# Queueing each PSUM eviction of the second-stage groups with the group's last product instead of with the next unit of work

## The chip, the cores and the metric

One core of a Trainium2 chip. The kernels of the first four experiments ran on one chip and those of the last on another, each beside the kernel before. The metric is the device time of one launch in microseconds, of which several runs are given. All runs quoted here are of the fast state.

## The reference, cut to what matters

Softcapped attention (batch 8, 12 heads, 448 rows, head size 64), followed by a two-branch maximum and an output product:

```python
scores = cap * np.tanh(scale * np.matmul(q, k.transpose(0, 1, 3, 2)) / cap)   # cap = 30
attn = np.exp(scores - max) / sum
x = np.matmul(attn, v)  ->  (3584, 768)
g = np.maximum(x @ w1, x @ w2)          # w1, w2: (768, 1024)
out = g @ w_out                         # w_out: (1024, 768)
```

The kernel uses max(a, b) = max(a - b, 0) + b: `g` becomes relu(x @ (w1 - w2)), and x @ w2 @ w_out is added through a premultiplied matrix `wm`.

## The kernel before

TensorE writes its products into banks of the memory called PSUM. A *group* is the products that are summed up in one bank, and its *eviction* is the VectorE instruction that copies the sum out, after which the bank can take another group. In the listings `esum` holds sums of exponentials, `xT` the result of attention, `gT` the relu results and `osb` finished output rows; `st`, `rs` and `inv` are the three steps from the softmax sum to its inverse.

The kernel interleaves two stages. The first (attention) keeps ScalarE busy with tanh and exp. The second (`moe`) is pure matrix work and fills the gaps of TensorE: it is a Python generator, and `F(n)` takes n products from it wherever the first stage leaves room. All engines get their instructions in the order in which the Python code records them.

```python
mm_psum = ctx.enter_context(tc.tile_pool(name="mm_psum", bufs=2, space=PSUM))   # two banks for "mm"
...
def moe(b):
    ...
    for f in range(FC):                                  # 8 groups of 6 products
        ps = mm_psum.tile([P, 512], f32, name="mm")
        for c in range(KC):
            nc.tensor.matmul(ps[:, :S], wd_sb[:, c, ...], x[:, c, cs], ...)      # L399
            yield
        nc.vector.tensor_relu(g[:, f, cs], ps[:, :S])                            # L403, the eviction
    for t in ...:
        for half in range(2):                            # groups of 14 products
            ps = mm_psum.tile([P, 512], f32, name="mm")
            ...                                          # L411 and L414, a yield after each product
            nc.vector.tensor_copy(osb[:, hs], ps[:, : DM // 2])                  # L418, the eviction
...
def F(n):
    rate[1] += n * rate[0]
    while rate[1] >= 1 and fill_q:
        try:
            next(fill_q[0])
            rate[1] -= 1
        except StopIteration:
            fill_q.pop(0)
...
for t in range(1, NQ):                                   # one pass is about 12 us
    ...                                                  # F, scores, exp, additions to esum
    F(3); add(t, 0, 2)
    F(4); add(t, 1, 2)
    F(8)
    scores(t + 1, 2); ex(t + 1, 1)
    total(t)                 # PE L350: sum of esum; VectorE: st L352, rs, inv
    normalize(t, values(t))  # PE L366/L372: v; VectorE: two multiplications to xT, L387
    F(9)
```

The `yield` comes after each product. So after the last product of a group the generator pauses, and the eviction is recorded only when the next unit is taken: behind whatever the loop has recorded for VectorE between two calls of `F`. This happens only where a group's last product is also the last of a call of `F`.

## Time and profile before

| | before |
|---|---|
| median of 3 runs | 347.99 us (347.97 to 348.53) |
| span of the profiled run | 345.9 us |
| TensorE (PE) busy | 94% |
| ScalarE (ACT) busy | 80% |
| VectorE (DVE) busy | 66% |

How to read it: PE is the busiest engine, so what counts is the time in which PE stands still. The prediction below shows the lines for that. Two more views carry the argument. The first is what ACT waited for from 210 us to 302 us in the kernel before (us in total, times, longest): it has gaps, so it follows PE and does not lead it.

```profile
ACT tanh L304 <- PE s L303: 3.4, 6, 1.3
ACT tanh L304 <- PE s L300: 0.2, 1, 0.2
```

The second is PE's timeline near 175 us in the kernel before (start, length, what, count).

```profile
173.47 4.76 PE L399 MATMUL mm<-xT,wd_sb 128*128 128x448 bf16 x22
```

22 products at 189 ns each, the last one shown with its 353 ns, would be 21 x 0.189 + 0.353 = 4.32 us. It takes 4.76, so some 0.44 us are stalls within one line that shows no idle mark. By the starts of the single records they are 0.145 us at 175.32 and 0.284 us at 177.87. I call this "lost time": the distance between the starts of two products less 189 ns (448 columns) or 163 ns (384).

The same measure finds another loss, which is no wait for an eviction. In the kernel before PE passes 116 times from 72 us to the end between products of form 128\*128 and products of form 64\*128 or 128\*32, and each time 92 to 96 ns are lost without an idle mark: 10.9 us in all, about three times the stalls that this document is about. No experiment here touches them.

### The profile page before, as it was taken

The page shows a single profiled execution, that of the slowest core. Times are in us where ns is not written, and L with a number is a line of the kernel's source. Part 1 is how long each engine was busy: PE and PEld are TensorE (multiplying, and loading weights), DVE is VectorE, ACT ScalarE, POOL GpSimd, SP SyncE. Part 2 cuts the span into 40 slices and gives each one's busy share as a digit, 9 for nine tenths or more (in the row PEclk, how much of TensorE's full clock was granted, in tenths as well). Part 3 has the DMA queues.
Part 4 walks back from the last instruction along what each step waited for, and adds up shares of the span by engine and source line. Part 5 has one row for each costly group of instructions (what it writes and reads, how often), then busy time and mean ns, then how long its engine had stood idle before and what let it go on. Part 6 is the DMA issues. An engine that isn't in the chain of part 4 may idle for free.

```text
span 345.9 us, 6777 instructions
## 1 busy us (share of the span) xinstructions
PE 326.2 (94%) x2710; PEld 163.3 (47%) x2710; DVE 227.4 (66%) x410; ACT 277.2 (80%) x241; POOL 109.8 (32%) x172
## 2 busy tenths in 40 slices
PE   3669979999999999999999999999999999999996
PEld 1324545445544554455444454454445554555563
DVE  5324645886777767777687768767776777874421
ACT  3998939989999999899999999799989999900000
POOL 6653848542144134304413431341343040000000
PEclk9959999999999999999999999999999999999999
DMA  7999999997695969775985499839956921012032
GB/s 253 252 253 242 369 204 180 247 213 199 132 295 158 211 149 282 205 172 123 252 252 100 134 230 300 179 96 216 307 124 143 209 96 46 2 47 91 0 93 91
DMA packets 103200, 61.78 MB, mean 179 GB/s; under 512 B 62337, under 2 KB 98177, under 8 KB 103169
## 3 DMA queue, kind: packets, MB, share of 16 engines
q1 hardware_dynamic: 101216, 58.21, 65.1%
q0 software_dynamic: 1952, 3.15, 5.0%
q8 instruction: 21, 0.34, 0.4%
q14 instruction: 11, 0.08, 0.1%
HBM read 42.47 MB, written 11.01 MB: 155 GB/s over the span
## 4 chain that ended last, share of the span: by engine, by line
PE 80%; DMA 13%; DVE 5%; issue 1%; SPq 0%; DVEq 0%
PE mm L414 22%; PE mm L399 19%; PE mm L411 16%; DMA kr<-in_k_dram 9%; PE v L366 6%; PE s L303 6%; DMA qkT<-kqf 3%; PE v L303 2%; PE s L300 2%; PE v L372 2%; PE mm L243 2%; PE s L350 2%; DMA osb<-in_moe_w_dram 1%; DVE xT L387 1%; DVE gT L403 1%; DVE st L352 1%
## 5 line engine op out<-in xcount | busy, mean ns | idle before, releaser
L309 ACT ACTIVATE expo<-tanh 128x2688 bf16<-128x2688 bf16 (+1 forms) x72 | 140.3, 1950 | 0.8 <-PE v L366 0.6
L304 ACT ACTIVATE tanh<-s 128x896 bf16<-128x896 f32 x122 | 106.4, 914 | 24.3 <-PE s L303 20.2
L414 PE MATMUL mm<-wo_sb,gT 128*128 128x384 bf16 x448 | 85.8, 327 | 0.0
L399 PE MATMUL mm<-xT,wd_sb 128*128 128x448 bf16 x384 | 78.8, 353 | 1.9 <-DVE gT L403 1.4
L411 PE MATMUL mm<-wm_sb,xT 128*128 128x384 bf16 x336 | 66.0, 326 | 0.4 <-DVE gT L403 0.4
L414 PEld LDWEIGHTS <-gT 128*128 128x128 bf16 x448 | 42.3, 98 | 34.7 <-issue 8.5
L418 DVE COPY osb<-mm 128x384 f32<-128x384 f32 x56 | 31.1, 555 | 40.7 <-PE mm L414 40.3
L399 PEld LDWEIGHTS <-wd_sb 128*128 128x128 bf16 x384 | 35.8, 98 | 41.2 <-issue 11.0
L403 DVE TENSOR_SCALAR gT<-mm 128x448 bf16<-128x448 f32 x64 | 39.4, 622 | 17.7 <-PE mm L399 17.2
L628 POOL COPY mark<-inv 1x1 f32<-1x1 f32 x18 | 3.2, 177 | 141.0 <-DVE inv L356 125.7
L411 PEld LDWEIGHTS <-xT 128*128 128x128 bf16 x336 | 31.7, 98 | 25.9 <-issue 5.9
L304 ACT ACTIVATE tanh<-v 128x896 bf16<-128x896 f32 x46 | 42.5, 923 | 0.0
L366 PE MATMUL v<-expo,vp 128*32 128x448 bf16 x576 | 35.6, 353 | 0.0
L303 PE MATMUL s<-qkT 64*128 64x448 bf16 x196 | 29.1, 371 | 6.7 <-ACT tanh L304 3.1
L387 DVE TENSOR_TENSOR xT<-v,inv 128x448 bf16<-128x448 f32 x48 | 27.8, 620 | 4.4 <-PE v L372 2.0
L352 DVE STREAM_TRANSPOSE st<-s 128x448 f32<-128x448 f32 x24 | 15.6, 650 | 19.8 <-PE s L350 17.5
L329 DVE TENSOR_TENSOR esum<-expo 128x896 bf16<-128x896 bf16 x42 | 27.9, 665 | 0.0
L327 DVE TENSOR_TENSOR esum<-esum,expo 64x896 bf16<-64x896 bf16 x42 | 26.6, 633 | 1.3
L331 DVE TENSOR_TENSOR esum<-esum,expo 128x896 bf16<-128x896 bf16 x42 | 26.7, 637 | 1.0
L303 PEld LDWEIGHTS <-qkT 64*128 64x128 bf16 x288 | 10.6, 96 | 29.7 <-issue 21.3
L366 PEld LDWEIGHTS <-vp 128*32 128x32 bf16 x576 | 15.3, 97 | 10.0
L183 POOL CAST kqf<-kr 128x1152 bf16<-128x1152 f32 x14 | 15.9, 1137 | 10.5 <-DMA kr<-in_k_dram 10.3
(66 smaller groups left out, 257.1 us busy)
## 6 DMA issues: line engine op xcount, KB each, us to landing
kr<-in_k_dram SPq DMA_DIRECT2D x14, 576.0 KB, 7.2
qr<-in_q_dram SPq DMA_DIRECT2D x14, 576.0 KB, 7.0
vr<-in_v_dram SPq DMA_DIRECT2D x14, 576.0 KB, 4.9
out_dram<-osb SPq DMA_DIRECT2D x20, 384.0 KB, 3.5
out_dram<-osb SPq DMA_DIRECT2D x16, 192.0 KB, 3.3
osb<-in_moe_w_dram SPq DMA_DIRECT2D x4, 512.0 KB, 8.6
gT<-in_moe_w_dram POOLq DMA_DIRECT2D x6, 256.0 KB, 12.8
wo_sb<-in_moe_w_out_dram POOLq DMA_DIRECT2D x4, 384.0 KB, 16.0
```

What stands on the lines that cost most here:

```text
L303: nc.tensor.matmul(s[:, m, :S], k0[r, j * P : (j + 1) * P], qTn[r, :])
L304: nc.scalar.activation(tanh[t, p][:, 2 * j : 2 * j + 2, :], s[:, :, :S], AF.Tanh, scale=scale / cap)
L309: nc.scalar.activation(expo[t, p], tanh[t, p][:, 0:n, :], AF.Exp, scale=float(cap))
L329: nc.vector.tensor_add(d, e_of(t, ab, 0), e_of(t, ab, 1))
L331: nc.vector.tensor_add(d, d, e_of(t, ab, 2))
L366: nc.tensor.matmul(ps[r, :S], vp[g % 2][:, 2 * n + h, j, u::2], e_of(t, ab, j)[:, h, :], start=(j == 0), stop=False,)
L387: nc.vector.tensor_mul(x_of(t, u), ps[:, u, :S], inv[t])
L399: nc.tensor.matmul(ps[:, :S], wd_sb[:, c, f * P : (f + 1) * P], x[:, c, cs], start=(c == 0), stop=(c == KC - 1))
L403: nc.vector.tensor_relu(g[:, f, cs], ps[:, :S])
L411: nc.tensor.matmul(ps[:, : DM // 2], x[:, c, ts], wm_sb[:, c, hs], start=(c == 0), stop=False)
L414: nc.tensor.matmul(ps[:, : DM // 2], g[:, f, ts], wo_sb[:, f, hs], start=False, stop=(f == FC - 1))
L418: nc.vector.tensor_copy(osb[:, hs], ps[:, : DM // 2])
```

## The change

Its intent: the eviction is recorded together with the group's last product, so that VectorE can empty the bank as soon as the group is done. The same edit is made in the three generators; the core of it:

```diff
     def moe(b):
+        yield
         ...
         for f in range(FC):
-            ps = mm_psum.tile([P, 512], f32, name="mm")
             for c in range(KC):
+                if f + c > 0:
+                    yield
+                if c == 0:
+                    ps = mm_psum.tile([P, 512], f32, name="mm")
                 nc.tensor.matmul(...)
-                yield
             nc.vector.tensor_relu(g[:, f, cs], ps[:, :S])
     ... (the same in turn_w2, premultiply and the second half of moe)
     def F(n):
         rate[1] += n * rate[0]
         while rate[1] >= 1 and fill_q:
+            g = fill_q[0]
+            if g is not rate[2]:
+                rate[2] = g
+                next(g)
+            rate[1] -= 1
             try:
-                next(fill_q[0])
-                rate[1] -= 1
+                next(g)
             except StopIteration:
                 fill_q.pop(0)
```

More of the change, by code (lines that the diff above doesn't have):

```diff
@@ L229, in turn_w2 @@
     def turn_w2(c):
-        ps = mm_psum.tile([P, 512], f32, name="mm").bitcast(bf16)
         for f in range(FC):
+            yield
+            if f == 0:
+                ps = mm_psum.tile([P, 512], f32, name="mm").bitcast(bf16)
             nc.tensor.transpose(ps[:, f * P : (f + 1) * P], w2b[:, c, f * P : (f + 1) * P], ident)
-            yield
         w2T[c] = stage.tile([P, FC * P], bf16, name="w2T", bufs=2)
@@ L240, in premultiply @@
             hs = slice(half * (DM // 2), (half + 1) * (DM // 2))
-            ps = mm_psum.tile([P, 512], f32, name="mm")
             for f in range(FC):
+                yield
+                if f == 0:
+                    ps = mm_psum.tile([P, 512], f32, name="mm")
                 nc.tensor.matmul(
@@ L246, in premultiply @@
                 )
-                yield
             nc.vector.tensor_copy(wm_sb[:, c, hs], ps[:, : DM // 2])
@@ L391, in moe @@
     def moe(b):
+        yield
         if b % 2 == 0:
@@ L396, in moe @@
         for f in range(FC):
-            ps = mm_psum.tile([P, 512], f32, name="mm")
             for c in range(KC):
+                if f + c > 0:
+                    yield
+                if c == 0:
+                    ps = mm_psum.tile([P, 512], f32, name="mm")
                 nc.tensor.matmul(
@@ L401, in moe @@
                 )
-                yield
             nc.vector.tensor_relu(g[:, f, cs], ps[:, :S])
@@ L408, in moe @@
                 hs = slice(half * (DM // 2), (half + 1) * (DM // 2))
-                ps = mm_psum.tile([P, 512], f32, name="mm")
                 for c in range(KC):
+                    yield
+                    if c == 0:
+                        ps = mm_psum.tile([P, 512], f32, name="mm")
                     nc.tensor.matmul(ps[:, : DM // 2], x[:, c, ts], wm_sb[:, c, hs], start=(c == 0), stop=False)
+                for f in range(FC):
                     yield
-                for f in range(FC):
                     nc.tensor.matmul(
@@ L416, in moe @@
                     )
-                    yield
                 nc.vector.tensor_copy(osb[:, hs], ps[:, : DM // 2])
@@ L440 @@
     fill_q = []
-    rate = [1.0, 0.0]
+    rate = [1.0, 0.0, None]
     def F(n):
```

## The prediction

> **What bounds the kernel now.** I read first the page's busy table and slices (which engine is full, and when), then the waits of TensorE (what it stands still for), then the timeline of TensorE and VectorE around its longest wait, and then that of two smaller stalls which the wait view hides.
>
> ```profile
> PE 326.2 (94%) x2710; PEld 163.3 (47%) x2710; DVE 227.4 (66%) x410; ACT 277.2 (80%) x241; POOL 109.8 (32%) x172
> ...
> PE   3669979999999999999999999999999999999996
> ...
> DVE  5324645886777767777687768767776777874421
> ACT  3998939989999999899999999799989999900000
> ```
>
> TensorE (PE) is at 9 tenths or more from the fourth slice on but for the sixth and the last; VectorE (DVE), which does the evictions, is at about two thirds. ScalarE (ACT) is nearly as full as PE until about 302 us and then has nothing left, while PE goes on alone for 43 us. So the end is set by PE's total work plus every time PE stands still. Where does it stand still after the start? This is the view of PE's waits from 56 us to the end:
>
> ```profile
> PE mm L399 <- DVE gT L403: 1.4, 3, 0.8
> PE mm L411 <- DVE gT L403: 0.4, 1, 0.4
> PE mm L399 <- DVE xT L387: 0.2, 1, 0.2
> ```
>
> The columns are us in total, times, longest. Two microseconds in 290: that is about all that an earlier eviction could buy, and the change can only take the part that comes from the place of an eviction in the queue. The longest is at 217.75 us. First PE, then DVE, from the timeline (start, length, engine, line, count):
>
> ```profile
> 209.92 3.57 PE L399 MATMUL mm<-xT,wd_sb 128*128 128x448 bf16 x18
> 213.33 0.54 PE L300 MATMUL s<-qkT 128*128 128x448 bf16 x2
> 213.80 0.37 PE L350 MATMUL s<-esum,ones 128*32 128x448 bf16 x4
> ...
> 215.62 1.31 PE L399 MATMUL mm<-xT,wd_sb 128*128 128x448 bf16 x6
> 217.75 0.73 PE L399 MATMUL mm<-xT,wd_sb 128*128 128x448 bf16 x3 [0.82 <-DVE gT L403]
> ```
>
> ```profile
> 212.57 0.62 DVE L403 TENSOR_SCALAR gT<-mm 128x448 bf16<-128x448 f32 x1
> 214.23 0.65 DVE L352 STREAM_TRANSPOSE st<-s 128x448 f32<-128x448 f32 x1 [1.03 <-PE s L350]
> 214.91 0.24 DVE L354 RECIPROCAL rs<-st 128x14 f32<-128x14 f32 x1
> 215.26 0.65 DVE L356 STREAM_TRANSPOSE inv<-rs 128x448 f32<-128x448 f32 x1
> 216.01 1.16 DVE L387 TENSOR_TENSOR xT<-v,inv 128x448 bf16<-128x448 f32 x2
> 217.08 1.15 DVE L403 TENSOR_SCALAR gT<-mm 128x448 bf16<-128x448 f32 x2
> ```
>
> A group of L399 has 6 products. The 18 from 209.92 are three whole groups, the third of them done at 209.92 + 3.57 = 213.49. VectorE then idles 1.03 us and does not evict it: the eviction was not yet on its queue, because the generator had paused after the sixth product. The four steps of the softmax sum and the two multiplications come first, and the eviction is the first of the pair at 217.08, 3.59 us late. There are two banks for "mm", so the six products from 215.62 use the other bank, and the seventh stands still until 217.75.
>
> **What the Trainium skill says.** "PSUM — Partial Sum Buffer", section "Engine vs sequencer instructions": VectorE's queue is strict first in, first out, so a place in the queue is a place in time. The trace agrees: done at 213.49, evicted at 217.08, with VectorE idle in between. The same page, "PSUM bank collisions raise a hardware error": TensorE must not write a bank while it is read, and software guards that, so the next but one group's first product waits for the eviction. The trace agrees: eviction over at 217.70 (half of 1.15 us after 217.08, with a few hundredths of overlap), product at 217.75. "TensorE: Matmul & The Clock Gate", section "Step-by-step: what each phase is for": products in a row are N/2.4 + 2.5 ns apart, so 189 ns for 448 columns and 162.5 for 384. The trace agrees: starting at 209.92 and 213.33, 18 products take 3.41 us, 189 ns each. "Perfetto Trace Analysis", section "Identifying the Most-Contended Engine": matmul busy time is a bad measure because matmuls are pipelined. Here too: the stall shows as 0.82 us idle, but the seventh product was due 189 ns after the sixth, whose shown length is 353 ns (the L399 row's mean), so PE lost 0.82 + 0.353 - 0.189 = 0.98 us.
>
> **The change part by part.** It adds no instruction: it moves the `yield` from after a product to before it, so that one step of the generator now ends behind the group's last product and takes the eviction with it. The budget counts as before: a generator's first step is now free, and its end falls into its last paid step. I built both kernels and laid their instruction orders side by side. PE, ACT, POOL and SP have the same instructions in the same order; so output stores and input loads do not change places. On VectorE 123 of 136 evictions stand where they stood. 13 move forward: 12 of them ahead of one `esum` addition (0.62 us each), and one, of a gT group, ahead of the five steps from st to xT. That one is the eviction above.
>
> - *The one at 217.08.* Its group is done at 213.49. The eviction before it (212.57) will run slightly later, as another gT eviction moves ahead of an addition and waits for its group until 211.22: eviction 211.26 to 211.88, two additions to about 213.06, the eviction of 212.57 until about 213.65, and ours until about 214.2, about when st could start before (214.23). So it fits into the idle 1.03 us. The bank is free at 214.2 and wanted at 215.62 + 6 x 0.189 = 216.75. The stall vanishes: 217.75 - 216.75 = 1.0 us, 0.98 by the reckoning above.
> - *Two gT evictions at 174.65 and 295.36.* Both groups are done 0.44 us before their evictions start, because VectorE is in an addition. In the second, VectorE and then PE:
>
> ```profile
> 294.82 0.62 DVE L331 TENSOR_TENSOR esum<-esum,expo 128x896 bf16<-128x896 bf16 x1
> 295.36 1.35 DVE L403 TENSOR_SCALAR gT<-mm 128x448 bf16<-128x448 f32 x2
> ```
>
> ```profile
> 294.17 3.15 PE L399 MATMUL mm<-xT,wd_sb 128*128 128x448 bf16 x15
> ```
>
>   15 products would take 14 x 0.189 + 0.353 = 3.00 us and take 3.15, so PE lost 0.15. With the eviction ahead of L331 it starts at about 294.96 and that is won: the group that can then start earlier is evicted at 297.92, and no product waits for that. At 174.65 the same 0.15 would be won, but is given back: two groups on, PE waits for the eviction of 177.20, which stands behind two additions in both kernels. Net 0.
> - *The ten others* (eight of osb, two of gT). Each starts within 0.04 to 0.64 us of its group's end, and its bank is wanted 0.3 to 3.8 us after it is over. No PE time hangs on them: 0.
> - *Stalls that stay*: those at 68.2, 73.3, 95.7 to 96.3, 145.4 and 177.9 belong to evictions or xT steps which do not move.
>
> Sum: 0.98 + 0.15 = 1.13 us. It carries to the end only if nothing else binds behind 217 us. ACT's waits there speak for it: it waits for PE 3.6 us in 7 pieces, the longest (1.3 us) for just the product that comes 0.98 us earlier; PE never waits for ACT in that stretch. So ACT moves along. From 220 to 302 us PE shows 82.00 of 82.00 us busy. 347.99 - 1.13 = 346.9 us.
>
> **The rivals.** (1) *The early eviction blocks.* In 11 of the 13 moves the eviction has to wait for a group which ends after the addition could have started (by only 0.1 us in two of them); at 87.2, 196.4 and 244.6 the addition started 1.9, 1.6 and 1.7 us before the eviction, and will now come after it. If that pushed the softmax sum, PE's L350 would wait. Against it: behind each such move there is idle time before the next hard date (0.77, 1.27, 0.76 us in these three, against one addition of 0.62), and the sum's last addition is done 0.4 us or more before L350 wants it at 190.3, 238.6 and 262.9; only at 308.3 is it about 0.1 us. If I am wrong in one or two places, 0.2 to 0.6 us are lost, and the result is 347.3 to 347.9. (2) *ACT or a transfer takes over the bound.* If ACT had no slack, the 0.98 us would only become a wait of PE for a score bank, and would be given back: 347.8. ACT's waits speak against it; so do the key and query transposes, issued at 219.6 and landed 5.5 us later, while their scores come a pass of 12 us later. (3) *Much more comes out*, because evictions as such hold PE up: then 340 or less. The waits speak against it: all of them together are 2 us as shown, and 3.7 by the reckoning with 189 ns.
>
> **Range and chances.** Only 1.13 us is at stake and runs of one kernel spread by 0.5 us (347.97 to 348.53). I take 346.9, range 346.0 to 347.9: the low end allows for a spread of that size and a little more won; the high end is everything given back. Two per cent would be 7 us, more than all stalls behind 56 us: faster 0.01, within 2% 0.98, slower 0.01.
>
> **What would show it.** PE's waits behind 90 us should lose their entry of 0.8 us; the seventh L399 product near 217.7 should follow the sixth in one run without an idle mark. A gT eviction should stand at about 213.6, before st. The run of 15 near 293 should take 3.00 us. PE's busy time should hardly change and the span fall by 1.1 us. A new wait of PE for esum (L350), or a wait of PE for tanh, would prove me wrong, and so would a st that starts later against PE's products.

## The result, and the profile after

| | before (one run more than above) | after |
|---|---|---|
| median | 348.26 us (347.97 to 348.86, 4 runs) | 347.07 us (346.88 to 347.16, 4 runs) |
| ratio of fast runs | | 0.9963, 95% interval 0.9946 to 0.998 |
| span of the profiled run | 345.9 us | 345.3 us |

Ratios here are those of the record, from the fast runs, and not quite the ratio of the medians quoted. The change is worth 1.2 us by the medians; the interval of the ratio allows 0.7 to 1.9 us.

The changed kernel's lines are numbered differently: L399 became L405, the eviction L403 became L408, L411 and L414 became L418 and L421, st is L354, the sum L352. PE's waits from 56 us to the end, after:

```profile
PE mm L405 <- DVE gT L408: 0.7, 2, 0.4
PE mm L418 <- DVE gT L408: 0.4, 1, 0.4
PE mm L405 <- DVE xT L389: 0.2, 1, 0.2
```

The entry of 0.8 us is gone. Two smaller differences hide in the first line: 0.26 us near 178 us are new (see below), and the 0.18 us that were marked at 68.19 us before are missing. The latter is not the change's doing, as the first eviction that moves stands at 87 us: the lost time at that product was between 0 and 0.48 us in the eight traces of this case. The stretch in which the 0.8 us lay, PE and then DVE in the timeline of the changed kernel:

```profile
210.51 3.57 PE L405 MATMUL mm<-xT,wd_sb 128*128 128x448 bf16 x18
213.91 0.54 PE L302 MATMUL s<-qkT 128*128 128x448 bf16 x2
...
216.21 1.88 PE L405 MATMUL mm<-xT,wd_sb 128*128 128x448 bf16 x9
```

```profile
212.38 1.26 DVE L329 TENSOR_TENSOR esum<-esum,expo 64x896 bf16<-64x896 bf16 x2
213.68 1.16 DVE L408 TENSOR_SCALAR gT<-mm 128x448 bf16<-128x448 f32 x2
214.81 0.65 DVE L354 STREAM_TRANSPOSE st<-s 128x448 f32<-128x448 f32 x1
```

What stood as 6 products, a stall and 3 products is one run of 9: 8 x 0.189 + 0.353 = 1.87 us are expected and 1.88 shown. The eviction is the second of the pair at 213.68; VectorE has no idle time left before st, so it fits in with nothing to spare. The run of 15 that took 3.15 us in the kernel before takes 3.01, with its eviction at 294.56 ahead of the addition; the run of 22 near 174 us keeps a stall, and that one now has an idle mark of its own:

```profile
293.78 3.01 PE L405 MATMUL mm<-xT,wd_sb 128*128 128x448 bf16 x15
```

```profile
174.05 4.15 PE L405 MATMUL mm<-xT,wd_sb 128*128 128x448 bf16 x21
178.46 0.35 PE L405 MATMUL mm<-xT,wd_sb 128*128 128x448 bf16 x1 [0.26 <-DVE gT L408]
```

21 products without a stall are 20 x 0.189 + 0.353 = 4.13 us: the first stall is gone. The second lost 0.284 us before and loses 0.425 now, so 0.141 of the 0.145 us that the first one won were given back.

**Why the two profiles' spans differ by 0.6 us only.** The start of a run varies: the 601st of PE's 2710 matmul records began at 72.00 us in the profile before and at 72.59 in the one after, on the same instructions. The traces show where the 0.59 us come from. The granted TensorE clock, at half in both, came back to full at 27.53 us before and only at 29.42 after. These are the same two products, before and then after; by their single records their starts are 189 and 374 ns apart:

```profile
27.98 0.54 PE L300 MATMUL s<-qkT 128*128 128x448 bf16 x2
```

```profile
28.36 0.95 PE L302 MATMUL s<-qkT 128*128 128x448 bf16 x2
```

Just before the stall near 68 us PE was 0.91 us behind, and 0.32 us of it were won back at that stall. What sets the moment at which the clock comes back is not shown. From the 601st record to the start of the last it is 270.16 us before and 269.03 after: 1.12 us less (differences of this kind are taken before rounding), where 1.13 were predicted. In what follows I call this stretch "from the 601st product on". It is the sharper measure: in the second trace of the changed kernel, on another occasion, it was 269.03 us again.

### The profile page after: what moved, and what is told of

It reads as the page before. It is cut to its first block, busy times and chain, and to the rows that moved or that the text cites. A ratio compares the mean times of both kernels' runs of the same rounds, so it can differ in the third digit from the quotient of the medians.

```text
span 345.3 us, 6777 instructions
## 1 busy us (share of the span) xinstructions
PE 326.7 (95%) x2710; PEld 163.6 (47%) x2710; DVE 226.5 (66%) x410; ACT 277.1 (80%) x241; POOL 107.8 (31%) x172
## 3 DMA queue, kind: packets, MB, share of 16 engines
q0 software_dynamic: 1952, 3.15, 5.0%
## 4 chain that ended last, share of the span: by engine, by line
PE 81%; DMA 13%; DVE 4%; issue 0%; SPq 0%; DVEq 0%
PE mm L421 22%; PE mm L405 20%; PE mm L418 16%; DMA kr<-in_k_dram 9%; PE v L368 6%; PE s L305 6%; DMA qkT<-kqf 3%; PE v L305 2%; PE s L302 2%; PE v L374 2%; PE mm L246 2%; PE s L352 2%; DMA osb<-in_moe_w_dram 2%; DVE xT L389 1%; DVE gT L408 1%; DVE st L354 1%
## 5 line engine op out<-in xcount | busy, mean ns | idle before, releaser
L421 PE MATMUL mm<-wo_sb,gT 128*128 128x384 bf16 x448 | 85.8, 327 | 0.0
L405 PE MATMUL mm<-xT,wd_sb 128*128 128x448 bf16 x384 | 78.3, 353 | 1.0 <-DVE gT L408 0.7
L418 PE MATMUL mm<-wm_sb,xT 128*128 128x384 bf16 x336 | 66.1, 327 | 0.4 <-DVE gT L408 0.4
L421 PEld LDWEIGHTS <-gT 128*128 128x128 bf16 x448 | 42.3, 98 | 34.7 <-issue 8.5
L405 PEld LDWEIGHTS <-wd_sb 128*128 128x128 bf16 x384 | 35.8, 98 | 39.6 <-issue 8.6
L408 DVE TENSOR_SCALAR gT<-mm 128x448 bf16<-128x448 f32 x64 | 39.3, 621 | 16.9 <-PE mm L405 16.7
L418 PEld LDWEIGHTS <-xT 128*128 128x128 bf16 x336 | 31.7, 98 | 25.9 <-issue 5.9
L354 DVE STREAM_TRANSPOSE st<-s 128x448 f32<-128x448 f32 x24 | 15.6, 649 | 16.3 <-PE s L352 14.0
```

Of the source, the lines that this page charges most:

```text
L405: nc.tensor.matmul(ps[:, :S], wd_sb[:, c, f * P : (f + 1) * P], x[:, c, cs], start=(c == 0), stop=(c == KC - 1))
L418: nc.tensor.matmul(ps[:, : DM // 2], x[:, c, ts], wm_sb[:, c, hs], start=(c == 0), stop=False)
L421: nc.tensor.matmul(ps[:, : DM // 2], g[:, f, ts], wo_sb[:, f, hs], start=False, stop=(f == FC - 1))
```

## The experiments

The kernels below were built so that PE, ACT, POOL and SP have the same instructions in the same order as before; only VectorE's order differs, and the traces show the same. For the first three I put every eviction into a function which either records it at once, or at the next unit as before (`LATE`), or after `normalize` of the same pass (`HOLD`). Evictions are numbered as they are recorded. With all 13 moved ones in `LATE` every engine's order, as built, is that of the kernel before; with none it is that of the changed kernel (neither was run). In these kernels L447 is L399, L450 is the eviction L403 and L460 is L411. The edit, shortened:

```diff
-            nc.vector.tensor_relu(g[:, f, cs], ps[:, :S])
+            evict(lambda f=f, ps=ps: nc.vector.tensor_relu(g[:, f, cs], ps[:, :S]))
+    def evict(f):
+        n = count[0]; count[0] += 1
+        if n in LATE: waiting.append(f)      # recorded when the next unit is taken
+        elif n in HOLD: held.append(f)       # recorded after normalize(t, ...)
+        else: f()
```

The theory is that of the prediction: an eviction's place costs PE time only where its bank is wanted before the eviction is over, and of the 13 moves one wins 0.98 us, one 0.15, one wins 0.15 and loses it again, and ten nothing. The main rival is that evicting earlier helps a little everywhere.

### One move alone

```diff
+    LATE = {27, 53, 62, 69, 71, 76, 87, 89, 98, 105, 111, 116}    # all that moved but number 78
```

> Theory (one eviction pays): this is the kernel before with only the single gT eviction moved that stood behind the five steps from st to xT. PE's 0.8 us wait for L403 near 217 us goes, the others stay, and the time falls by 0.98 us: ratio to before 0.997. Rival (evictions at the group's end help in general, a little at each of 13 places): one of 13 gives about 0.1 us, ratio 0.9997.

Measured: 347.40 us median of 17 runs, before 348.43 of 30 on the same chip; ratio 0.9973, interval 0.9962 to 0.9983. From the 601st product on it took 269.18 us, 0.97 less than the kernel before. PE's waits from 56 us on:

```profile
PE mm L447 <- DVE gT L450: 0.4, 1, 0.4
PE mm L460 <- DVE gT L450: 0.4, 1, 0.4
PE mm L447 <- DVE xT L406: 0.2, 1, 0.2
```

The 0.8 us entry is gone with this one move, and 0.983 us of lost time with it (the mark near 68 us, which varies, is missing here too); the lost times of 0.148, 0.281 and 0.146 us near 176, 179 and 296 us are as in the kernel before. The interval excludes the rival's 0.9997.

### The other twelve moves

```diff
+    LATE = {78}
```

> Theory: the other twelve moves without that one. PE's 0.8 us wait stays. The moves near 175 and 295 us each win 0.15 us, the first is given back about 3 us later at the next wait for a gT eviction (that wait grows from 0.28 to 0.43 us of lost time), so net 0.15 us: ratio 0.9996. Rival (general help): nearly the whole gain of the change, ratio 0.9965 to 0.997. Rival (early evictions in part block VectorE): slower than before by 0.2 to 0.6 us, ratio 1.001 to 1.002.

Measured: 348.24 us, ratio 0.9988, interval 0.9973 to 1.0003. The times alone do not tell 0.9996 from 1, but they exclude both rivals' values (0.9965 to 0.997, and 1.001 to 1.002). The trace tells the rest: 270.02 us from the 601st product on, 0.14 less than before.

```profile
218.83 0.73 PE L447 MATMUL mm<-xT,wd_sb 128*128 128x448 bf16 x3 [0.82 <-DVE gT L450]
```

In this view of PE's timeline the 0.82 us stall stands as it did. The lost time near 296 us is gone; near 176 us it is gone and near 179 us it is 0.425 instead of 0.284. So twelve of the thirteen moves together are worth one gain of 0.14 us, as the theory has it.

### The same cost made four times over

```diff
+    HOLD = {36, 49, 93, 106}      # in the changed kernel; flushed after normalize(t, values(t))
```

> The suspected cost made larger: the changed kernel with four more gT evictions (at t = 6, 8, 17, 20) held back until behind the two multiplications of the same step, as the one was in the kernel before. Theory: lost PE time is the end of the held eviction less the moment its bank is wanted in the trace of the changed kernel: 1.92, 1.74 less 0.60 of a stall it swallows, 1.56 and 1.36, together 6.0 us: 353.1 us, ratio to before 1.014, and four waits of PE for L408-like evictions of 1 us and more. Rival (ScalarE or the DMA sets the pace there, PE's stalls are partly absorbed): less than 3 us more than the changed kernel.

Measured: 353.26 us, ratio 1.0138, interval 1.0119 to 1.0157. From the 601st product on: 274.99 us, 5.96 more than the changed kernel, where the theory said 6.0. The four lost times by the records are 1.92, 1.74, 1.55 and 1.36 us (predicted 1.92, 1.74, 1.56, 1.36). The first of them in PE's timeline, and in VectorE's the pair of evictions whose first one it waits for:

```profile
111.05 1.14 PE L460 MATMUL mm<-wm_sb,xT 128*128 128x384 bf16 x6 [1.75 <-DVE gT L450]
```

```profile
109.31 1.16 DVE L406 TENSOR_TENSOR xT<-v,inv 128x448 bf16<-128x448 f32 x2
110.38 1.15 DVE L450 TENSOR_SCALAR gT<-mm 128x448 bf16<-128x448 f32 x2
```

This is the picture of the kernel before at 217 us, made on purpose. As practically all of it reached the end, neither ScalarE nor a transfer absorbs PE's stalls at these four places, from 111 to 294 us: that rival falls.

### Three more evictions forward

Three of the stalls that remain, near 74, 146 and 178 us, belong to evictions which the change does not move, because the first stage's VectorE work is recorded ahead of the group's last product. Here that work is put behind it:

```diff
-        normalize(t, values(t))
+        ps = values(t)
+        if t in (3, 9):
+            F(2)
+        normalize(t, ps)
...
-        F(9)
+        F(7 if t in (3, 9) else 9)
...
         F(4)
+        if t == 12:
+            F(2)
         add(t, 1, 2)
...
-        F(8)
+        F(6 if t == 12 else 8)
```

> The changed kernel with three more evictions moved forward: at t = 3 and 9 two products and the eviction they end are queued before the two multiplications, at t = 12 one addition comes behind the eviction of the group that is then ending. Theory: the stalls near 74, 146 and 178 us go, 0.53 + 0.60 + 0.43 = 1.56 us: 345.5 us, ratio to before 0.992. Rival (the later multiplications or addition hold up the next scores or sums): nothing won or lost against the changed kernel, ratio 0.9965 or more.

Measured: 345.83 us (6 runs), ratio 0.9923, interval 0.9904 to 0.9942. The three stalls are gone from the view of waits:

```profile
PE mm L405 <- DVE xT L389: 0.2, 1, 0.2
```

But from the 601st product on it took 267.81 us, 1.22 less than the changed kernel and not 1.56. Record by record the lost times fell by 0.531, 0.601 and 0.425, and at two places behind t = 3 and 9 they rose, by 0.162 and 0.137. The first of the two shows in the timeline of PE's weight loads, and its cause in VectorE's:

```profile
73.74 0.10 PEld L305 LDWEIGHTS <-qkT 64*128 64x128 bf16 x2 [0.44 <-DVE xT L389]
```

```profile
72.00 0.62 DVE L408 TENSOR_SCALAR gT<-mm 128x448 bf16<-128x448 f32 x1 [0.38 <-PE mm L405]
72.55 1.15 DVE L389 TENSOR_TENSOR xT<-v,inv 128x448 bf16<-128x448 f32 x2
```

The next scores are written to the bank pair of the values, of which there is one. The two multiplications read it, and they had been pushed back behind the eviction. The rival was right in part: an eviction forward is a multiplication back.

### The eviction between the two multiplications

```diff
     def normalize(t, ps):
         for u in range(2):
+            if t in (3, 9) and u == 1:
+                F(2)
             nc.vector.tensor_mul(x_of(t, u), ps[:, u, :S], inv[t])
```

It takes the place of the `F(2)` ahead of `normalize` and was run beside the changed kernel once more.

> The changed kernel once more, beside the next one on the same chip. Theory: the gain of the prediction's sum, 1.13 us, ratio to before 0.997; between its 600th and its last recorded product on PE 269.0 us as in its first trace.

> The changed kernel with three evictions moved as in three_more, but at t = 3 and 9 the two products and their eviction are queued between the two multiplications instead of before both. In three_more the scores that go to the bank pair of the values then waited 0.16 and 0.14 us for the later multiplication. Theory: with the first multiplication run while the group is ending, the second is over about 0.3 us sooner, so these two waits go too: 600th to last product on PE 267.5 us (267.8 in three_more, 269.0 in the changed kernel), ratio to before 0.992. Rival: the second multiplication is still too late and 267.8 stays, or the eviction is now late and the stalls near 73 and 145 us come back in part.

Measured: the changed kernel 347.12 us, ratio 0.9959 (0.9946 to 0.9973); this one 345.47 us (6 runs), ratio 0.9902 (0.9868 to 0.9936). From the 601st product on: 269.03 and 267.56 us. VectorE's timeline at t = 3:

```profile
72.00 0.62 DVE L391 TENSOR_TENSOR xT<-v,inv 128x448 bf16<-128x448 f32 x1
72.54 0.61 DVE L410 TENSOR_SCALAR gT<-mm 128x448 bf16<-128x448 f32 x1
73.07 0.61 DVE L391 TENSOR_TENSOR xT<-v,inv 128x448 bf16<-128x448 f32 x1
```

The first multiplication runs while the group is still ending, so the second is over sooner: 1.23 us after the start of the 601st product, where it was 1.52 in the experiment before. Both waits of the scores are gone; of the three stalls, 0.530, 0.527 and 0.424 us were won, and 0.074 us are left near 145 us. ("600th" in the expectations is the record counted from zero, the 601st here.) This version beats both kernels: 2.9 us below the kernel before by the medians, 1.65 below the changed one. It is tied to the places of these sizes, though: the passes 3, 9 and 12 were read from the trace.

## Why the prediction was right

It said 346.9 us; 347.07 was measured. The time alone would prove little, as the range of 346.0 to 347.9 reaches almost to the kernel before; the traces decide. By the prediction's own steps:

- *What bounds the kernel.* PE's work plus PE's stalls, with nothing to absorb them. The four held evictions show it: 6.0 us of stalls were to come in, 5.96 arrived.
- *The one eviction behind five steps: 0.98 us.* Right. Alone it took away a stall of 0.983 us and gave 0.97 us from the 601st product on. It fits in ahead of st as worked out: st began 0.43 us after the sum's first product before (214.23 less 213.80) and 0.42 after (214.81 less 214.39).
- *Two gT evictions behind one addition: 0.15 us and nothing.* Right. The other twelve moves gave 0.14 us in all, and the stall which gives the second gain back grew from 0.284 to 0.425 us.
- *Ten moves worth nothing, and blocked additions that cost nothing.* Right together: the twelve moves show no other change of 20 ns or more than these, and PE's sums (L350) got no new wait. Each of the ten by itself was not run.
- *Rival 2, ScalarE or a transfer takes over.* It fell with the held evictions. Rival 3, a general gain, fell with the two halves of the change.
- *Two per cent.* There were 3.7 us of such stalls behind 56 us in all, so it could not be reached by moving evictions; the best version takes 2.6 us of them from the 601st product on (270.16 less 267.56).

One thing of its list of signs did not come as said: the span of the profiled run fell by 0.6 us and not by 1.1. The mechanism was not at fault: the 601st product began 0.59 us later in that run, mostly because the granted clock stayed at half for longer near 28 us, before any eviction that moved. The prediction had left such differences at the start of a run out of that sign.

## What to carry to other kernels

Ask of each PSUM eviction three moments: when its group is done, when it starts, and when its bank is wanted again; only where the third comes before the eviction's end is there anything to win, and the difference is what is won, as long as the engine that waits sets the end. Here 123 of 136 evictions did not move, ten of the 13 that moved won nothing, and one made most of the gain. When you move one forward, ask the same three moments of what you put behind it.

## What the Trainium skill lacked or had wrong

- "TensorE: Matmul & The Clock Gate", section "Back-to-back issue gap", gives 131 ns per product for N = 512 in a stream of weight loads and products, and calls N/2.4 + 2.5 ns the gap of an isolated product, too long for a stream at large N. Here each product has its own weight load, and the records are 189 ns apart at 448 columns and 162 to 163 ns at 384: the formula, not less (no product here has 512 columns).
- "Perfetto Trace Analysis", section "Tensor Engine Instruction (MATMUL, LD_WEIGHTS)", says that TensorE's end times are a model, but not what that does to a stall: idle marks understate each one by the shown length less the true distance (353 less 189 = 164 ns at 448 columns). 0.82 us shown were 0.98 lost, and 0.145 us lost had no mark at all.
- "Perfetto Trace Analysis", section "Matmuls", says to rotate groups through PSUM banks so that the eviction of one overlaps the products of the next. It does not say that this holds only if the eviction also stands early enough in its engine's queue: with two banks in turn, four evictions put behind five other steps cost 5.96 us.
- "TensorEngine Tiling (Array Packing)" has no figure for what a change of the form costs: in the kernel before 116 changes between 128\*128 and 64\*128 or 128\*32 lost 92 to 96 ns each.
